# Twelve token-tile pairs by 7 products instead of nine, ScalarE copies for the turns, and row loads behind a landed turn, in an attention and feed-forward kernel on one core

## The chip, the cores and the metric

The kernel runs on one core of a Trainium2 chip. The metric is device time in microseconds (us) of one execution. A core has TensorE (PE: matmuls, into the 8 banks of PSUM), VectorE (DVE), ScalarE (ACT), GpSimd (POOL), SyncE (SP), each with its own in-order queue, and 16 DMA engines that all of them share. SP's queue issues the stores of results and the transposing DMAs, POOL's queue issues the loads.

## The reference

```python
def _attn_ref(q, k, v):            # 8 batches, 12 heads, 448 rows, 64 columns
    scale = 1.0 / np.sqrt(q.shape[-1])
    scores = scale * np.matmul(q, k.transpose(0, 1, 3, 2))
    attn = np.maximum(scores, 0.0) ** 2 / q.shape[2]
    return np.matmul(attn, v)

def _moe_ref(x, w_in, w_out, alpha):   # x: 3584 tokens x 768; w_in 768 x 2048; w_out 2048 x 768
    h = x @ w_in
    g = np.maximum(h, 0.0) + alpha * np.minimum(h, 0.0)
    return g @ w_out
```

The heads' outputs, side by side, are x. All inputs and the result are float32 in memory; the kernel computes in bf16 and sums in float32.

## The kernel before

A **group** n is four heads of one batch (three groups a batch, 24 in all). Its q and k rows are loaded (`load_qk`, L112), its v rows by `load_v` (L121). q and k must be turned, so that the head's 64 columns lie on partitions: groups 0 to 4 by matmuls with the identity (`turn_pe`), groups 5 to 23 by `turn_dma` (L185): two copies put the rows in order into `perm` (one buffer for all; groups 5, 7 and 8 borrow memory of `w_mix`), and one transposing DMA from SP writes T. The copies are made by DVE up to n = 11 and by POOL from n = 12 on (L192, `GP`).

**Scores** of a group come in 7 chunks of two banks each. `sc` (L253) multiplies a chunk (`score_mm`, L206), has its relu taken out of PSUM by ACT ("A", L215) or DVE ("D", L217), and puts the chunk on a list, `late`. `sq(k)` squares the first k of that list on DVE (L228). `attnv(n)` (L231) multiplies all 7 squared chunks with v into two banks; ACT and DVE each take one into xT (L248, L249). `burst(n)` is some chunks of a later group, attnv(n), and some more chunks; PA, PB and PC (L559 to L561) are its patterns of engines, FB is three chunks at ff = 9.

**f1** of a batch b has 16 steps ff: six matmuls of 448 columns (L272), `neg` by ACT (L280, two buffers), gT = neg x beta + h by DVE (L281), and one square from `late`. gT holds the activations of two batches (896 tokens, 7 tiles of 128), `sb` = b // 2 being the number of these two.

**The output** gT @ w_out is made in one of two ways. A *direct* tile, `f2(sb, c, h)` (L298): 16 matmuls of 256 columns for h = 0, 16 of 512 for h = 1, copied out by ACT (L307), stored by SP. A *pair* of tiles, class `Pair` (L320): the 256 tokens x 2048 times 2048 x 768 as a 2 x 2 block product in 7 products (p1 to p7) of 8 matmuls with 384 columns (L340). It needs four mixes S of gT for each pair (`mix`, L336, DVE), four mixes of w_out made once (`weight_mix`, L318, DVE, in halves) and seven drains, five of them sums on DVE (L345), two copies on ACT (p1, p2).

The order is written out by hand. After b = 1 (L608 to L635) come the 7 direct tiles of batches 0 and 1, with score chunks, weight mixes, and bursts 6 to 8 between them. Then the loop over b from 2 to 7 (L638): f1 with the turns of two groups at ff = 1 and 9, then the output stage. For even b that is the pair (0, 1) and the direct tile 2 of its two batches, for odd b the pairs (3, 4) and (5, 6). Between the products stand the three bursts of the batch, and `prepare(n0 + 4)` behind the first of them. `prepare(n)` turns group n and loads all rows of group n + 2.

PSUM banks are given by a counter in program order (`take_bank`, `take_pair`: the least recently taken, from b = 2 on filled pair by pair; `hold` keeps a bank back). A matmul into a bank waits until the bank's last reader is done, so a late DVE or ACT instruction comes back to PE as a wait some banks later.

Of the kernel before, what the change touches and what calls it, by code (L numbers as in the profile page):

```python
# [11 lines left out]
BF16 = mybir.dt.bfloat16  # L12
# [1 line left out]
ALU = mybir.AluOpType  # L14

PP = 64
GP = 12
NJ = 7


# [1 line left out]
def kernel(  # L22
# [28 lines left out]
    rl_pool = ctx.enter_context(tc.tile_pool(name="rl", bufs=6))  # L51
    at_pool = ctx.enter_context(tc.tile_pool(name="at", bufs=10))
    xT_pool = ctx.enter_context(tc.tile_pool(name="xT", bufs=2))
    g_pool = ctx.enter_context(tc.tile_pool(name="g", bufs=1))
    neg_pool = ctx.enter_context(tc.tile_pool(name="neg", bufs=2))
    o_pool = ctx.enter_context(tc.tile_pool(name="o", bufs=6))
    u_pool = ctx.enter_context(tc.tile_pool(name="u", bufs=2))
# [124 lines left out]
            copy = nc.vector.tensor_copy if eng == "D" else nc.scalar.copy  # L182
            copy(dst, ps[:, 128 * lo:128 * hi])  # L183

    def turn_dma(n):  # L185
        if n in (5, 7, 8):
            w = w_mix[2 + n % 2].rearrange("p k c -> p (k c)")[:, :4 * NJ * D]
            p = w.rearrange("p (a j s d) -> p a j s d", a=2, j=NJ, s=2)
        else:
            p = perm_pool.tile([128, 2, NJ, 2, D], BF16, tag="perm", name="perm")  # L190
        for i, name in enumerate("qk"):
            (nc.gpsimd if n >= GP else nc.vector).tensor_copy(p[:, i], raw.pop((n, name)).rearrange("p s j d -> p j s d"))  # L192
        t = T_pool.tile([128, 2, NJ, 128], BF16, tag="T", name="T")
        nc.sync.dma_start_transpose(out=t.rearrange("p a j c -> p (a j) c"),
                                    in_=p.rearrange("p a j s d -> p (a j s d)"))
        T[n] = t
# [68 lines left out]
        sq()  # L265


    gT = {}

    def f1_mm(ps, b, ff, ks):  # L270
        for km in ks:
# [2 lines left out]
                             start=(km == 0), stop=(km == KM - 1))  # L274

    def f1_out(ps, b, ff):
        if b // 2 not in gT:
            gT[b // 2] = g_pool.tile([128, KF, 2 * S], BF16, tag="g", name="gT")
        neg = neg_pool.tile([128, S], F32, tag="neg", name="neg")
        nc.scalar.activation(neg, ps, ACTF.Relu, scale=-1.0)  # L280
        nc.vector.scalar_tensor_tensor(gT[b // 2][:, ff, (b % 2) * S:(b % 2) * S + S],  # L281
                                       neg, beta_sb[:, ff:ff + 1], ps, ALU.mult, ALU.add)
        sq(1)

# [13 lines left out]
    def f2(sb, c, h, parts=None):  # L298

        first_col, width = COLS[h][0], COLS[h][1] - COLS[h][0]  # L300
        o = o_pool.tile([128, d_model - CUT], F32, tag="o", name="osb")
        for lo, hi in parts or ((0, width),):
            ps = take_bank()[:, :hi - lo]
            for ff in range(KF):
                nc.tensor.matmul(ps, gT[sb][:, ff, bass.ts(c, 128)], w_out_sb[:, ff, first_col + lo:first_col + hi],  # L305
                                 start=(ff == 0), stop=(ff == KF - 1))
            nc.scalar.copy(o[:, lo:hi], ps)  # L307
            store(sb, c, first_col + lo, first_col + hi, o[:, lo:hi], nc.scalar if parts else nc.sync)
# [10 lines left out]

    class Pair:  # L320

        def __init__(self, sb, ta, tb):
            self.sb, self.ta, self.tb = sb, ta, tb
            ga, gb = gT[sb][:, :, bass.ts(ta, 128)], gT[sb][:, :, bass.ts(tb, 128)]
            self.a11, self.a12, self.a21, self.a22 = ga[:, :KH], ga[:, KH:], gb[:, :KH], gb[:, KH:]
            self.s = {}

# [30 lines left out]
        def p2(self):  # L358
            self.mm(self.x, self.a12, w_out_sb[:, KH:, :NH], False)
            t = o_pool.tile([128, d_model - CUT], F32, tag="o", name="osb")[:, :NH]  # L360
            nc.scalar.copy(t, self.x)
            take(self.xb, 1)
            store(self.sb, self.ta, 0, NH, t)

        def p6(self):
            y = take_bank()[:, :NH]
# [8 lines left out]
        def p5(self):  # L375
            self.zb = hold()
            self.z = psum[:, self.zb, :NH]
            self.mm(self.z, self.s[1], w_mix[0], True)
            store(self.sb, self.tb, NH, d_model, self.plus(self.z, self.u3))

        def p4(self, parts=((0, NH),)):
            for lo, hi in parts:
                y = take_bank()[:, :hi - lo]
                self.mm(y, self.a22, w_mix[3][:, :, lo:hi], True)
                t = self.plus(y, self.u3[:, lo:hi])
                store(self.sb, self.tb, lo, hi, t, nc.scalar if len(parts) > 1 else nc.sync)

        def p3(self):
            self.mm(self.z, self.s[4], w_out_sb[:, KH:, NH:], False)
            store(self.sb, self.ta, NH, d_model, self.plus(self.z, self.u2))  # L390
            take(self.zb, 1)


# [112 lines left out]
        for ff in range(lo, hi):  # L506
            f1(b, ff)

    def load(n):
        if n < NQ:  # L510
            load_qk(n)
            load_v(n)

    def prepare(n):
        if n < NQ:
            turn_dma(n)
        load(n + 2)

    f1s(0, 4, 6)
    sc(ch(3, 0, 3))  # L520
# [6 lines left out]
    f1_out(ps, 0, 9)  # L527
    f1s(0, 10, 12)
    sc(ch(3, 6, 7) + ch(4, 0, 2, "AA"))
    turn_dma(5)  # L530
    f1s(0, 12, 13)
    kept = late[:]
    del late[:]
# [33 lines left out]
        at_c[0] = min(lo + k, len(chunks))  # L567
        return [(n, j, e) for (n, j), e in zip(chunks[lo:at_c[0]], p)]

    def burst(n, before="ADA", after="AD", squares=True):  # L570

        sc(some(len(before), before))
        attnv(n)
        sc(some(len(after), after))
        if squares:
            sq()

    early = []
    for ff in range(5):
        early.append(hold())  # L580
        f1_mm(psum[:, early[ff], :S], 1, ff, range(4))
        if ff == 1:
            sc(ch(5, 5, 7))
            sq(1)
            sq(1, "A")
        if ff == 3:
            attnv(5)
            turn_dma(6)
            nc.gpsimd.tensor_copy(landed, T[6][:1, 0, 0, :1])
            load_w_out(1, 4)  # L590
            load_qk(9)
            load_v(6)
            load_v(7)
    for ff in range(KF):
        if ff < 5:
            f1_mm(psum[:, early[ff], :S], 1, ff, range(4, KM))
            f1_out(psum[:, early[ff], :S], 1, ff)
            take(early[ff], 1)
        else:
            f1(1, ff)  # L600
        if ff in (1, 10):
            turn_dma(7 + ff // 9)
        if ff == 10:
            nc.gpsimd.tensor_copy(landed, T[8][:1, 0, 0, :1])
            load_v(8)
            load_v(9)
            load(10)
    f2(0, 3, 0)  # L608
    run(some(3))
    f2(0, 4, 0)  # L610
    run(some(3))
    f2(0, 0, 1)
    prepare(9)
    f2(0, 1, 1)
    run(some(3))
    weight_mix(0, 0, 4)
    f2(0, 5, 0)
    burst(6)
    f2(0, 2, 1)
    weight_mix(0, 4, 8)  # L620
    weight_mix(1, 0, 4)
    run(some(3))
    f2(0, 3, 1)
    weight_mix(1, 4, 8)
    f2(0, 6, 0)
    prepare(10)
    burst(7)
    weight_mix(2, 0, 4)
    f2(0, 4, 1)
    weight_mix(2, 4, 8)  # L630
    f2(0, 5, 1)
    weight_mix(3, 0, 4)
    burst(8)
    f2(0, 6, 1)
    weight_mix(3, 4, 8)  # L635

    paired.append(1)
    for b in range(2, B):  # L638
        n0 = NG * (b + 1)
        last = b == B - 1  # L640
        sb = b // 2
        for ff in range(KF):
            if not last:
                if ff in FB:
                    sc(some(*FB[ff]))
                if ff in (1, 9):
                    prepare(n0 + 2 + ff // 8)
            f1(b, ff)
        if b % 2 == 0:
            p = Pair(sb, 0, 1)  # L650
            f2(sb, 2, 0)
            p.mix(1, 2)
            burst(n0, *PA, False)
            p.mix(3)
            p.p1()
            sq(4)
            prepare(n0 + 4)
            p.p6()
            sq(1)
            p.p7()  # L660
            p.mix(4)
            p.p2()
            sq(1)
            p.p5()
            sq(1)
            p.p4()
            p.p3()
            burst(n0 + 1, *PB)
            f2(sb, 2, 1)
            burst(n0 + 2, *PC, False)  # L670
        else:
            p, r = Pair(sb, 3, 4), Pair(sb, 5, 6)
            p.p1()
            p.mix(1, 2)
            r.p1()
            p.mix(3)
            r.mix(1)
            p.p2()
            sq()
            if not last:  # L680
                r.p2()
                burst(n0, *PA, False)
                prepare(n0 + 4)
                sq(3)
            p.p6()
            sq(1)
            p.p7()
            p.mix(4)
            p.p5()
            r.mix(2)  # L690
            p.p4()
            sq(1)
            p.p3()
            if not last:
                burst(n0 + 1, *PB, False)
            r.mix(3)
            sq(2)
            r.p6()
            sq(2)
            r.p7()  # L700
            r.mix(4)
            r.p5()
            if last:
                r.p2()
                r.p3()
                r.p4(((0, 256), (256, 384)))
            else:
                sq(1)
                r.p4()
                sq()  # L710
                r.p3()
                burst(n0 + 2, *PC, False)

# [29 lines left out]
```

## Time and profile before

| | |
|---|---|
| median of 3 runs | 380.89 us (380.72 to 382.02) |
| the profiled execution | 382.1 us, of which 380.1 us from the first to the last instruction (the span) |
| DVE squares L228 | 162, 98.3 us, mean 645 ns |
| DVE gT L281 | 128, 85.3 us, mean 677 ns |
| ACT relu of scores L215 | 135, 115.9 us, mean 929 ns |
| DVE relu of scores L217 | 33, 35.9 us, mean 1088 ns |
| turn copies L192 on DVE | 14, some 613 ns each |
| turn copies L192 on POOL | 24, mean 1011 ns (q) and 1193 ns (k) |
| transposing DMAs, issue to landing | 4.0 / 5.5 / 13.4 us (min, median, max of 19) |
| POOL's waits for T<-perm at L192 | 106.3 us in 12 waits |

The profile page gives for each engine the time that it was busy and its share of the span. A row of a group of instructions is: line, engine, operation, output and inputs, how many, busy time, mean ns of one. The chain of waits follows the work that ended last back from the end: each piece has its start, its length and what it was. A row of the timeline has the start, the length, engine, line and what it wrote and read, and in brackets how long the engine idled before it and for whom. In a table by stage each row has the stretch, its length, and the busy time of PE, PE's weight loads (PEld), DVE, ACT and POOL with the count of instructions, then the granted clock, the DMA share and GB/s. Stretches used below start and end where PE turns from one stage to the next.

### The profile page before, as it was taken

The numbers are of one execution on the slowest core, as the hardware profiler recorded it, in microseconds if no ns is written. First come the engines' busy times: TensorE is split into PE (matmuls) and PEld (weight loads), VectorE is DVE, ScalarE is ACT, GpSimd is POOL, SyncE is SP. The second block draws the span as 40 slices with busy tenths as digits, with TensorE's granted clock in tenths as the row PEclk, the third lists the DMA queues.
The fourth block names the chain that finished last, engine by engine and source line by source line (L and its number), as shares of the span: only waits on it lengthen the run. The fifth ranks groups of instructions, "written<-read, shape, count | busy, mean of one in ns | idle before, by whom it ended". The sixth has DMA issues, their size and how long they took to land.

```text
span 380.1 us, 7810 instructions
## 1 busy us (share of the span) xinstructions
PE 367.7 (97%) x3112; PEld 204.3 (54%) x3112; DVE 288.4 (76%) x466; ACT 217.2 (57%) x339; POOL 94.1 (25%) x129
## 2 busy tenths in 40 slices
PE   7799999999999999999999999999999999999995
PEld 5454564555545455554655546554565546655553
DVE  2997988886988498777688779657879678756752
ACT  4988786556345653856644666576454766364400
POOL 8566050506210434043040430424011000000000
PEclk9999999999999999999999999999999999999999
DMA  9999989999996587859277686747062500220033
GB/s 142 199 203 202 178 132 192 165 195 176 225 178 116 96 135 109 154 92 111 56 130 144 81 117 108 140 93 122 1 96 62 108 2 14 60 53 0 1 85 84
DMA packets 73556, 43.28 MB, mean 114 GB/s; under 512 B 40368, under 2 KB 72240, under 8 KB 73520
## 3 DMA queue, kind: packets, MB, share of 16 engines
q0 software_dynamic: 27136, 22.58, 41.4%
q1 hardware_dynamic: 45952, 19.91, 26.9%
q8 instruction: 24, 0.39, 0.4%
q10 hardware_dynamic: 432, 0.30, 0.3%
q14 instruction: 12, 0.10, 0.1%
HBM read 45.62 MB, written 11.01 MB: 149 GB/s over the span
## 4 chain that ended last, share of the span: by engine, by line
PE 83%; DVE 11%; ACT 3%; issue 2%; POOL 0%; ACTq 0%; POOLq 0%
PE psum L272 31%; PE psum L340 21%; PE psum L305 14%; PE psum L238 9%; PE psum L206 8%; DVE at L228 5%; DVE gT L281 4%; ACT rl L215 2%; PE psum L180 1%; PE psum L164 1%; DVE rl L217 1%; DVE osb L345 1%; ACT xT L248 0%; ACT neg L280 0%; DVE T L183 0%
## 5 line engine op out<-in xcount | busy, mean ns | idle before, releaser
L272 PE MATMUL psum<-xT,w_in_sb 128*128 128x448 bf16 x768 | 148.9, 353 | 0.2
L215 ACT ACTIVATE rl<-psum 128x896 bf16<-128x896 f32 x135 | 115.9, 929 | 31.7 <-PE psum L206 22.4
L281 DVE SCALAR_TENSOR_TENSOR gT<-neg,beta_sb,psum 128x448 bf16<-128x448 f32 x128 | 85.3, 677 | 41.3 <-ACT neg L280 40.2
L272 PEld LDWEIGHTS <-w_in_sb 128*128 128x128 bf16 x768 | 73.9, 98 | 72.2 <-issue 4.8
L280 ACT ACTIVATE neg<-psum 128x448 f32<-128x448 f32 x128 | 68.9, 549 | 57.3 <-PE psum L272 39.8
L228 DVE TENSOR_TENSOR at<-rl 128x896 bf16<-128x896 bf16 x162 | 98.3, 645 | 0.2
L305 PE MATMUL psum<-w_out_sb,gT 128*128 128x256 bf16 (+1 forms) x320 | 54.7, 326 | 0.0
L206 PE MATMUL psum<-T 64*64 64x448 bf16 x672 | 47.6, 359 | 3.5 <-DVE gT L281 1.1
L217 DVE TENSOR_SCALAR rl<-psum 128x896 bf16<-128x896 f32 x33 | 35.9, 1088 | 13.3 <-PE psum L206 11.8
L305 PEld LDWEIGHTS <-gT 128*128 128x128 bf16 x320 | 30.4, 98 | 23.6 <-issue 3.8
L340 PEld LDWEIGHTS <-S 128*128 128x128 bf16 x288 | 28.0, 98 | 19.6 <-issue 1.2
L192 POOL COPY perm<-qraw 128x896 bf16<-128x896 bf16 x12 | 12.1, 1011 | 106.3 <-DMA T<-perm 106.3
L238 PE MATMUL psum<-at,vraw 64*64 64x448 bf16 x672 | 36.9, 350 | 0.8 <-DVE osb L345 0.8
L340 PE MATMUL psum<-w_mix,S 128*128 128x384 bf16 x216 | 37.2, 326 | 0.1
L206 PEld LDWEIGHTS <-T 64*64 64x64 bf16 x672 | 20.0, 106 | 23.5 <-issue 16.7
L238 PEld LDWEIGHTS <-vraw 64*64 64x64 bf16 x672 | 22.9, 106 | 12.4 <-issue 4.6
L340 PEld LDWEIGHTS <-gT 128*128 128x128 bf16 x224 | 21.6, 98 | 14.4 <-issue 0.9
L307 ACT COPY osb<-psum 128x256 f32<-128x256 f32 (+1 forms) x20 | 9.6, 479 | 30.9 <-PE psum L305 30.9
L340 PE MATMUL psum<-w_out_sb,gT 128*128 128x384 bf16 x144 | 25.0, 326 | 0.1
L125 POOL DMA_DIRECT2D vraw<-in_v_dram x24 | 17.4, 727 | 30.4 <-PE psum L206 28.1
L249 DVE TENSOR_SCALAR xT<-psum 128x448 bf16<-128x448 f32 x24 | 15.0, 624 | 11.9 <-PE psum L238 9.1
L345 DVE TENSOR_TENSOR osb<-psum,u 128x384 f32<-128x384 f32 (+2 forms) x28 | 15.2, 543 | 10.9 <-DMA out_dram<-osb 5.1
(44 smaller groups left out, 199.9 us busy)
## 6 DMA issues: line engine op xcount, KB each, us to landing
out_dram<-osb SPq DMA_DIRECT2D x70, 96.0 KB, 2.2
vraw<-in_v_dram POOLq DMA_DIRECT2D x24, 224.0 KB, 8.1
qraw<-in_q_dram POOLq DMA_DIRECT2D x23, 224.0 KB, 5.6
kraw<-in_k_dram POOLq DMA_DIRECT2D x23, 224.0 KB, 7.2
w_in_sb<-in_moe_w_in_dram POOLq DMA_DIRECT2D x16, 192.0 KB, 8.2
out_dram<-osb SPq DMA_DIRECT2D x20, 128.0 KB, 4.1
w_out_sb<-in_moe_w_out_dram POOLq DMA_DIRECT2D x4, 512.0 KB, 9.5
out_dram<-osb SPq DMA_DIRECT2D x21, 64.0 KB, 5.7
```

Of the source, the lines that this page charges most:

```text
L125: nc.gpsimd.dma_start(out=t.rearrange("p m j d -> p m (j d)"), in_=flat[:, 2 * g:2 * g + 2])
L206: nc.tensor.matmul(ps[64 * c:64 * c + 64, r, :S], t[64 * r:64 * r + 64, 1, j, 64 * c:64 * c + 64], t[64 * r:64 * r + 64, 0, :, 64 * c:64 * ...
L215: nc.scalar.activation(rl, ps[:, :, :S], ACTF.Relu)
L217: nc.vector.tensor_scalar(rl, ps[:, :, :S], 0.0, None, ALU.max)
L228: nc.vector.tensor_tensor(a, rl, rl, ALU.mult)
L238: nc.tensor.matmul(ps[64 * s:64 * s + 64, r, :S], vv[64 * r:64 * r + 64, s, j, :], a[64 * r:64 * r + 64, s], start=(j == 0), stop=(j == NJ ...
L272: nc.tensor.matmul(ps, w_in_sb[:, km // 2, km % 2, bass.ts(ff, 128)], xT[b][:, km // 2, km % 2, :], start=(km == 0), stop=(km == KM - 1))
L280: nc.scalar.activation(neg, ps, ACTF.Relu, scale=-1.0)
L281: nc.vector.scalar_tensor_tensor(gT[b // 2][:, ff, (b % 2) * S:(b % 2) * S + S], neg, beta_sb[:, ff:ff + 1], ps, ALU.mult, ALU.add)
L305: nc.tensor.matmul(ps, gT[sb][:, ff, bass.ts(c, 128)], w_out_sb[:, ff, first_col + lo:first_col + hi], start=(ff == 0), stop=(ff == KF - 1))
L340: nc.tensor.matmul(ps, left[:, i], right[:, i], start=(start and i == 0), stop=(i == KH - 1), skip_group_check=not start)
L345: nc.vector.tensor_tensor(t, ps, u, ALU.add)
```

## The change

- gT becomes one tile for the whole kernel, written in place, so that tiles of batch b can still be read while the next batch writes the other half. A `Pair` is now given as two (sb, tile) positions, which may lie in different pairs of batches.
- Twelve pairs instead of nine. Tiles 0, 1, 2 of the first two batches stay direct; (3, 4) and (5, 6) become pairs. The second of these is finished only in the output stage of b = 2: its S mixes are made at ff = 11 to 13, its products p6, p7, p5, p4, p3 come after f1. Every later batch but b = 5 has two pairs, among them one of tile 6 of batches 2 and 3 with tile 0 of batches 4 and 5, and so on; b = 5 has one pair and one direct tile.
- The copies of turns from n = 9 on are made by ACT; those of 5 to 8 stay on DVE. The turns inside f1 move from ff = 1 and 9 to ff = 4 and 12 (turn 8, in b = 1, from ff = 10 to 8).
- `prepare(n)` lets POOL read one element of T(n), so that its queue waits for the turn's landing, and then loads q and k of n + 2 and v of n + 1 (before: q, k and v of n + 2 at once). Around b = 1 loads are put behind turns by hand in the same way.
- Score chunks in the stage after b = 1 change their engines and places (three are moved into f1 of b = 1); squares are moved, among them one between the first chunks and attnv of burst PB (`mid`).

```diff
-GP = 12
...
-    g_pool = ctx.enter_context(tc.tile_pool(name="g", bufs=1))
...
 
-    def turn_dma(n):
+    def turn_dma(n, eng="A"):
         if n in (5, 7, 8):
             w = w_mix[2 + n % 2].rearrange("p k c -> p (k c)")[:, :4 * NJ * D]
             p = w.rearrange("p (a j s d) -> p a j s d", a=2, j=NJ, s=2)
         else:
             p = perm_pool.tile([128, 2, NJ, 2, D], BF16, tag="perm", name="perm")
         for i, name in enumerate("qk"):
-            (nc.gpsimd if n >= GP else nc.vector).tensor_copy(p[:, i], raw.pop((n, name)).rearrange("p s j d -> p j s d"))
+            (nc.vector.tensor_copy if eng == "D" else nc.scalar.copy)(p[:, i], raw.pop((n, name)).rearrange("p s j d -> p j s d"))
         t = T_pool.tile([128, 2, NJ, 128], BF16, tag="T", name="T")
...
-    gT = {}
+    gT = singles.tile([128, KF, 2 * S], BF16, name="gT")
...
     def f1_out(ps, b, ff):
-        if b // 2 not in gT:
-            gT[b // 2] = g_pool.tile([128, KF, 2 * S], BF16, tag="g", name="gT")
         neg = neg_pool.tile([128, S], F32, tag="neg", name="neg")
         nc.scalar.activation(neg, ps, ACTF.Relu, scale=-1.0)
-        nc.vector.scalar_tensor_tensor(gT[b // 2][:, ff, (b % 2) * S:(b % 2) * S + S],
+        nc.vector.scalar_tensor_tensor(gT[:, ff, (b % 2) * S:(b % 2) * S + S],
                                        neg, beta_sb[:, ff:ff + 1], ps, ALU.mult, ALU.add)
...
 
-        def __init__(self, sb, ta, tb):
-            self.sb, self.ta, self.tb = sb, ta, tb
-            ga, gb = gT[sb][:, :, bass.ts(ta, 128)], gT[sb][:, :, bass.ts(tb, 128)]
+        def __init__(self, a, b):
+            self.a, self.b = a, b
+            ga, gb = gT[:, :, bass.ts(a[1], 128)], gT[:, :, bass.ts(b[1], 128)]
             self.a11, self.a12, self.a21, self.a22 = ga[:, :KH], ga[:, KH:], gb[:, :KH], gb[:, KH:]
...
 
-    def load(n):
-        if n < NQ:
-            load_qk(n)
-            load_v(n)
-
     def prepare(n):
         if n < NQ:
             turn_dma(n)
-        load(n + 2)
+            nc.gpsimd.tensor_copy(landed, T[n][:1, 0, 0, :1])
+        if n + 2 < NQ:
+            load_qk(n + 2)
+        if n + 1 < NQ:
+            load_v(n + 1)
 
...
-    turn_dma(5)
+    turn_dma(5, "D")
...
 
-    def burst(n, before="ADA", after="AD", squares=True):
+    def burst(n, before="ADA", after="AD", squares=True, mid=0):
 
         sc(some(len(before), before))
+        sq(mid)
         attnv(n)
...
             attnv(5)
-            turn_dma(6)
+            turn_dma(6, "D")
             nc.gpsimd.tensor_copy(landed, T[6][:1, 0, 0, :1])
             load_w_out(1, 4)
-            load_qk(9)
             load_v(6)
-            load_v(7)
     for ff in range(KF):
...
             f1(1, ff)
-        if ff in (1, 10):
-            turn_dma(7 + ff // 9)
+        if ff == 9:
+            sc(some(3, "AAA"))
+        if ff in (1, 8):
+            turn_dma(7 + ff // 8, "D")
         if ff == 10:
             nc.gpsimd.tensor_copy(landed, T[8][:1, 0, 0, :1])
+            load_qk(9)
+            load_v(7)
+            load_qk(10)
             load_v(8)
-            load_v(9)
-            load(10)
-    f2(0, 3, 0)
-    run(some(3))
-    f2(0, 4, 0)
-    run(some(3))
+    p, r = Pair((0, 3), (0, 4)), Pair((0, 5), (0, 6))
+    p.p1()
+    run(some(3, "AAA"))
+    r.p1()
+    run(some(2, "AD"))
+    p.p2()
+    weight_mix(0, 0, 4)
+    r.p2()
+    weight_mix(0, 4, 8)
     f2(0, 0, 1)
-    prepare(9)
+    weight_mix(1, 0, 4)
+    burst(6, "ADA", "AA", False)
+    turn_dma(9)
+    nc.gpsimd.tensor_copy(landed, T[9][:1, 0, 0, :1])
+    load_qk(11)
+    load_v(9)
+    sq(3)
+    weight_mix(1, 4, 8)
     f2(0, 1, 1)
-    run(some(3))
-    weight_mix(0, 0, 4)
-    f2(0, 5, 0)
-    burst(6)
+    sq()
+    p.mix(1, 2)
+    weight_mix(2, 0, 4)
+    sc(some(3, "AAA"))
+    p.mix(3)
+    weight_mix(2, 4, 8)
     f2(0, 2, 1)
-    weight_mix(0, 4, 8)
-    weight_mix(1, 0, 4)
-    run(some(3))
-    f2(0, 3, 1)
-    weight_mix(1, 4, 8)
-    f2(0, 6, 0)
-    prepare(10)
-    burst(7)
-    weight_mix(2, 0, 4)
-    f2(0, 4, 1)
-    weight_mix(2, 4, 8)
-    f2(0, 5, 1)
+    sq()
+    burst(7, "ADA", "AA", False)
+    turn_dma(10)
+    nc.gpsimd.tensor_copy(landed, T[10][:1, 0, 0, :1])
+    load_qk(12)
+    load_v(10)
+    load_v(11)
     weight_mix(3, 0, 4)
-    burst(8)
-    f2(0, 6, 1)
+    sq(1)
+    p.p6()
     weight_mix(3, 4, 8)
+    sq(1)
+    p.p7()
+    p.mix(4)
+    p.p5()
+    sq(2)
+    p.p4()
+    sq(1)
+    p.p3()
+    burst(8, "ADA", "AAA", False)
 
     paired.append(1)
+    pairs = {3: (((1, 2), (1, 3)), ((1, 4), (1, 5))),
+             4: (((1, 6), (2, 0)), ((2, 1), (2, 2))), 6: (((2, 6), (3, 0)), ((3, 1), (3, 2))),
+             7: (((3, 3), (3, 4)), ((3, 5), (3, 6)))}
     for b in range(2, B):
...
                     sc(some(*FB[ff]))
-                if ff in (1, 9):
+                if ff in (4, 12):
                     prepare(n0 + 2 + ff // 8)
+            if b == 2 and ff == 8:
+                p, r = r, Pair((1, 0), (1, 1))
+            if b == 2 and 11 <= ff <= 13:
+                p.mix(ff - 10)
+            if b == 2 and ff == 14:
+                r.p1()
             f1(b, ff)
-        if b % 2 == 0:
-            p = Pair(sb, 0, 1)
-            f2(sb, 2, 0)
+        if b == 5:
+            p = Pair((sb, 3), (sb, 4))
+            f2(sb, 5, 0)
             p.mix(1, 2)
...
             burst(n0 + 1, *PB)
-            f2(sb, 2, 1)
+            f2(sb, 5, 1)
             burst(n0 + 2, *PC, False)
         else:
-            p, r = Pair(sb, 3, 4), Pair(sb, 5, 6)
-            p.p1()
-            p.mix(1, 2)
-            r.p1()
-            p.mix(3)
-            r.mix(1)
-            p.p2()
-            sq()
+            if b > 2:
+                p, r = [Pair(*t) for t in pairs[b]]
+                p.p1()
+                p.mix(1, 2)
+                r.p1()
+                p.mix(3)
+                r.mix(1)
+                p.p2()
+                sq()
+            else:
+                p.p6()
+                r.mix(1)
             if not last:
                 r.p2()
                 burst(n0, *PA, False)
                 prepare(n0 + 4)
                 sq(3)
-            p.p6()
+            if b > 2:
+                p.p6()
             sq(1)
...
             if not last:
-                burst(n0 + 1, *PB, False)
+                burst(n0 + 1, *PB, False, 1)
             r.mix(3)
...
             else:
-                sq(1)
+                sq(2)
                 r.p4()
-                sq()
                 r.p3()
```

(`store` and `f2` take the one gT and the pair's positions accordingly.)

More of the change, by code (lines that the diff above doesn't have):

```diff
@@ L304, in f2 @@
             for ff in range(KF):
-                nc.tensor.matmul(ps, gT[sb][:, ff, bass.ts(c, 128)], w_out_sb[:, ff, first_col + lo:first_col + hi],
+                nc.tensor.matmul(ps, gT[:, ff, bass.ts(c, 128)], w_out_sb[:, ff, first_col + lo:first_col + hi],
                                  start=(ff == 0), stop=(ff == KF - 1))
@@ L362, in p2 @@
             take(self.xb, 1)
-            store(self.sb, self.ta, 0, NH, t)
+            store(*self.a, 0, NH, t)
         def p6(self):
@@ L378, in p5 @@
             self.mm(self.z, self.s[1], w_mix[0], True)
-            store(self.sb, self.tb, NH, d_model, self.plus(self.z, self.u3))
+            store(*self.b, NH, d_model, self.plus(self.z, self.u3))
         def p4(self, parts=((0, NH),)):
@@ L385, in p4 @@
                 t = self.plus(y, self.u3[:, lo:hi])
-                store(self.sb, self.tb, lo, hi, t, nc.scalar if len(parts) > 1 else nc.sync)
+                store(*self.b, lo, hi, t, nc.scalar if len(parts) > 1 else nc.sync)
         def p3(self):
             self.mm(self.z, self.s[4], w_out_sb[:, KH:, NH:], False)
-            store(self.sb, self.ta, NH, d_model, self.plus(self.z, self.u2))
+            store(*self.a, NH, d_model, self.plus(self.z, self.u2))
             take(self.zb, 1)
```

## The prediction

> **What bounds the kernel now.** I read the busy times first, then the chain of waits from b=2 on, then busy time by stage, then single squares on VectorE.
>
> ```profile
> PE 367.7 (97%) x3112; PEld 204.3 (54%) x3112; DVE 288.4 (76%) x466; ACT 217.2 (57%) x339; POOL 94.1 (25%) x129
> PEclk9999999999999999999999999999999999999999
> ```
>
> TensorE (PE) works 367.7 of 380.1 us at the full granted clock. A busy PE need not be a useful PE, so I look at what it issues, in the chain of waits (start, length, what):
>
> ```profile
> 138.29 1.75 PE psum L305 x16
> ...
> 142.68 9.26 PE psum L340 x56
> ...
> 154.67 3.56 PE psum L305 x16
> ...
> 165.77 0.59 DVE gT L281
> 166.36 0.68 DVE at L228
> 167.04 0.59 DVE gT L281
> 167.63 0.54 DVE at L228
> ```
>
> Columns run at a fixed rate: 16 matmuls of 256 columns take 1.75 us, 16 of 512 take 3.56, 56 of 384 take 9.26 (0.165 each). A **direct** token tile costs 1.75 + 3.56 = 5.31, two cost 10.62, a **pair by 7 products** 9.26. The chain passes through VectorE (DVE) only in places: from 163.9 to about 172 it alternates gT and squares at 1.13 us per ff, beside six matmuls of 1.147 us. So PE sets the time, and DVE runs so close that each delay of it can show. The stages show where it does (length; busy PE, PEld, DVE, ACT, POOL):
>
> ```profile
> 76.53:119.17 42.64, 42.22 (x370) 22.06 (x368) 35.19 (x52) 21.03 (x31) 10.22 (x15) 1.00 1.20 189
> 119.17:138.13 18.96, 18.96 (x110) 9.57 (x109) 13.56 (x23) 10.96 (x19) 6.66 (x8) 1.00 0.55 99
> 138.13:161.05 22.92, 22.84 (x246) 13.74 (x245) 18.75 (x29) 13.82 (x21) 6.30 (x8) 1.00 0.77 132
> 161.05:181.05 20.00, 19.52 (x109) 9.77 (x108) 14.88 (x25) 12.57 (x21) 7.48 (x9) 1.00 0.77 105
> 181.05:208.63 27.58, 26.88 (x270) 16.21 (x268) 23.12 (x38) 13.99 (x21) 5.00 (x6) 1.00 0.58 109
> ...
> 271.16:298.15 26.99, 26.68 (x269) 16.14 (x267) 22.38 (x38) 13.99 (x21) 2.60 (x2) 1.00 0.39 70
> 298.15:317.51 19.36, 19.36 (x110) 9.81 (x110) 13.96 (x25) 12.55 (x21) 0.00 (x0) 1.00 0.17 35
> 317.51:338.90 21.39, 21.37 (x222) 12.56 (x220) 15.96 (x27) 11.62 (x17) 0.00 (x0) 1.00 0.19 44
> ```
>
> They are: the direct tiles after b=1; f1 and output of b=2; f1 and output of b=3; output of b=5; f1 and output of b=6. The same f1 with squares takes 20.0 in b=3 and 19.36 in b=6, the one in which POOL copies nothing.
>
> **Parts 1 and 2: the pairs.** Three direct pairs of tiles become 7-product pairs: 3 x (10.62 - 9.26) = **4.1 us of PE** less. It is moved work too. After b=1 go 4 x 1.75 + 7 x 3.56 = 31.9 and come 3 x 3.56 + 72 products x 0.165 = 22.6, so -9.3. b=2 has 96 products (40 left from the carried pair, 56 of its own) for 56 and a direct tile: 15.9 - 14.6 = +1.3. b=4 and b=6 trade a direct tile for a pair, +3.95 each; b=5 does the opposite, -3.95. Sum -4.1 again.
>
> DVE gains 12 S mixes x 0.687 and 15 sums x 0.557 = 16.6 us; six drains of scores (relu) that turn from D to A in the stage after b=1 take 6 x 1.088 = 6.5 off, three turns that leave it 6 x 0.613 = 3.7. Net +6.4 before part 3.
>
> Stage by stage, taking each new stage from one of its kind in this trace:
> - After b=1: 42.64 - 9.3 = 33.3. DVE: four weight_mix pairs 7.6, 27 squares less 3 and 6 that move into f1 = 18 x 0.62 = 11.2, four drains 4.4, xT 1.9, four mixes 2.7, five sums 2.8: 30.6, beside 33.3. It fits on the whole, but the last third doesn't: from burst(7) the sums, the last two mixes of weights and squares come one after another, while the products are 1.3 us each; burst(8)'s attnv waits for a square and a bank. Laid out in order I get about 1 us of waiting: **34.3**.
> - b=2: f1 18.96 plus r.p1 (1.3) plus 0.3 for squares that it lacked: 20.6. Output: the b=5 one less the three products not there, 26.99 - 3.9 = 23.1, plus 0.5 because gT of ff 15 comes later (three mixes at ff 11 to 13, turn copies at ff 12) and r.p2 waits for it: **44.2**.
> - b=3, b=4: f1 19.4, output 27.0 each: **92.8**.
> - b=5: 19.4 + 22.9 = **42.3**.
> - b=6: 19.4 + 27.0 less 1.5 for the scores that have run out (22.92 - 21.39): **44.9**.
>
> Together 258.5 against 338.90 - 76.53 = 262.4 before: **-3.9 us**. b=7 and all before b=1 is as it was.
>
> **Part 3: turn copies, from POOL (n >= 12) and DVE (n = 9 to 11) to ACT.** Thirty copies. ACT shows no SBUF copy of this size; the nearest row is its square of 128x896 bf16, 1009 ns; I take 1.0, so 2.0 a turn, at most 30 us on 217 (with six drains and the pairs about 250 of 376, 66%). Does ACT's queue delay anything? At ff=4 the neg of ff=4 waits behind them, then gT, then PE's bank. But neg already waits for gT two back, which runs at 1.13 us per ff: about 2.8 us between the end of one gT and the start of the third after it, against 0.55 + 2.0 + 0.55 = 3.1. It costs DVE 0.3, in the time before ff 6 to 8 where DVE has no squares. At ff=12 the copies come on top of three drains (ff 9, 2.5 us); nothing but neg is behind, and gT of ff 15 is due 3.7 us later (p1, r.p1, half of p2): nothing, except in b=2 (above). After PA, ACT is idle 4.65 us before PB: nothing. Without that cover the price is 2 us x 15 turns.
>
> What leaves is POOL's hold on DVE:
>
> ```profile
> 164.37 0.93 POOL L192 COPY perm<-qraw 128x896 bf16<-128x896 bf16 x1 [9.25 <-DMA T<-perm]
> ```
> ```profile
> 164.49 1.28 DVE L228 TENSOR_TENSOR at<-rl 128x896 bf16<-128x896 bf16 x1
> ...
> 167.56 0.61 DVE L228 TENSOR_TENSOR at<-rl 128x896 bf16<-128x896 bf16 x1
> ```
>
> A square beside the copy takes 1.28, the next without one 0.61. The Trainium skill, SBUF — State Buffer, section "SBUF: two separate sides", says that the pair of ports shared by DVE and GpSimd is locked for a whole instruction and the loser stops. By that rule 24 copies of some 1.1 us take up to 26 us from DVE. The rows give less: squares in b=2 to b=5, each stage against the same one of b=6 (0.62 and 0.56 each), lose 4.3 us in all, as DVE is waiting or reading PSUM for much of the time. On the end it is less still: PE's score group at ff=9 of b=3 lasts 1.74 us instead of 0.69, of b=6 0.94; that, and a square of 1.35 us ahead of PB, is what "19.4" above gives back. By the rule another 10 us could be hoped for; I go by the rows.
>
> **Part 4: rows fetched once a turn has landed.** `landed` on POOL waits for T, and load_qk(n+2), load_v(n+1) are behind it on POOL, which has nothing else left. SP's transpose now waits for ACT's copies instead of POOL's; stores behind it are freed sooner after PA (up to 5.4 us of POOL's wait for the buffer stood there). Landing of a transpose: median 5.5 us; 8.7 to 13.4 between 68 and 120 us with loads ahead of it, 4.0 to 8.2 afterwards. The Trainium skill, DMA: Bandwidth & Descriptors, section "Rules for kernel authors", speaks against the wait: issue DMAs early, and a transpose beside ordinary transfers needs nothing. By it the wait only makes rows later, by 4 to 6 us; by the rows it makes T earlier by up to 8. Either is hidden if rows land in time: from ff=4, 2.0 + 5 + 1.5 + 6 = 14.5 us, needed at the turn after PA, some 22 us later. After b=1 it is tight: T(8) lands near 82, rows 9 near 89, their turn near 90. Both 0 for the sum; the bounds go into the range (-0.5 to +2).
>
> **Sum.** The profiled execution took 382.1: span 380.1 and 2.0 around it. Span 376.2, that execution 378.2. It was 1.2 above the median of 380.89 (runs 380.72 to 382.02), so the forecast is 380.9 - 3.9 = **377.0**.
>
> **Rivals.**
> - *All of the waits go too.* PE's minimum says more than 4.1: score groups at ff=9 lose 1.05, 0.5, 1.0, 0.25 us over 0.69; outputs of odd batches lose 1 to 1.5. With POOL quiet some 2 to 3 us of these go beside the 4.1: **374.5**. For it: b=6's f1. Against: DVE's +6.4, and four stages with two pairs in place of two.
> - *DVE becomes the bound.* In the outputs with two pairs DVE is busy 22.4 to 23.1 us of 27, and the order of its queue, not its sum, sets PE's waits. If each of the new ones (b=2, 4, 6) and the stage after b=1 lose 0.8 more: +3.2, **380.2**, no difference.
> - *ACT waits for the transpose.* One perm buffer: a turn's copies wait until the last transpose has read it. On POOL that wait (106 us in all) stood beside nothing; on ACT, neg and drains are behind it. It decides once a transpose lands more than 7.8 us after issue: ff 4 to ff 12 is 9.9 us, less 2.0 for copies and 0.1. At 13.4, ACT stands 5.6 us, PE's banks cover some 3.4, 2.2 are lost in each of b=2 to b=6: +11, **388**. At 10 to 11, still 2 to 4 above the forecast. Against it: landings after 120 us are 4.0 to 8.2, and with the load behind it the 4.0 end is likelier.
> - *gT as one tile orders what it needn't*, if a write waits for readers of other columns. psum is also one tile and its banks run independently; counted within the second.
>
> **Chances.** Forecast 0.60, all waits 0.14, DVE 0.16, ACT 0.10. 0.5% (1.9 us) is about what a measurement of this kernel can tell from no change. Faster: the first two and a small part of the third, 0.77; same 0.13; slower 0.10. Low end: below 374.5 PE would need to lose nearly every wait; high end: the DVE case.
>
> **What would show it.** PE's busy sum falls by 4 to 5 us; L305 has 128 matmuls, L340 680 (8 more, as the last p4 goes in two parts). Squares have no 1.3 us outliers. Stage after b=1 near 34, b=2 near 44. Score groups at ff=9 near 0.95. ACT's wait for "DMA T<-perm" is near zero; if it isn't, or outputs of b=2, 4, 6 are over 28 us, the forecast is wrong.

## The result and the profile after

The changed kernel takes **375.62 us** (median of 4 runs, 375.11 to 376.17), the kernel before 381.45 (4 runs): ratio 0.9845, 95% interval 0.9812 to 0.9878. It is 5.8 us faster; the forecast was 3.9. A second comparison on another occasion gave 375.96 against 381.83, ratio 0.9842 (0.9821 to 0.9863). One execution each of e1 and e5 below took over 950 us (in e1's a matmul of f1 took 758 ns at the median instead of 352) and is left out.

The profiled execution has a span of 374.4 us, 5.7 less. Busy times of the changed kernel, to be read against the row of before:

```profile
PE 364.6 (97%) x3085; PEld 203.2 (54%) x3088; DVE 289.0 (77%) x481; ACT 242.1 (65%) x369; POOL 72.4 (19%) x120
```

PE still works at 97%. Of PEld, whose records are complete, there are 24 fewer, eight for each of three pairs. ACT has 25 us more, POOL 22 less, and DVE is where it was: what the three pairs gave it, the drains, the turns and POOL's silence took.

Busy time by stage, columns as before. The rows are the stage after b=1; f1 and output of b=2; f1 and output of b=3; f1 and output of b=5; f1 and output of b=6:

```profile
77.77:110.88 33.11, 32.65 (x300) 16.80 (x301) 28.63 (x44) 22.80 (x33) 8.57 (x14) 1.00 0.99 167
110.88:131.45 20.57, 20.57 (x116) 10.44 (x116) 15.53 (x28) 16.02 (x26) 4.03 (x7) 1.00 0.85 133
131.45:154.35 22.90, 22.84 (x246) 14.06 (x244) 20.36 (x35) 14.17 (x20) 5.04 (x8) 1.00 0.74 134
154.35:173.63 19.28, 19.28 (x108) 9.67 (x108) 13.91 (x25) 15.49 (x25) 2.33 (x4) 1.00 0.48 80
173.63:200.55 26.92, 26.80 (x270) 16.23 (x269) 22.61 (x38) 15.65 (x23) 4.66 (x8) 1.00 0.72 133
246.75:266.03 19.28, 19.28 (x108) 9.66 (x108) 13.91 (x25) 15.48 (x25) 2.33 (x4) 1.00 0.45 75
266.03:288.95 22.92, 22.80 (x244) 13.73 (x244) 17.82 (x29) 15.49 (x23) 3.22 (x6) 1.00 0.70 124
288.95:308.24 19.29, 19.29 (x109) 9.67 (x109) 13.89 (x25) 14.04 (x23) 0.18 (x1) 1.00 0.14 27
308.24:333.74 25.50, 25.44 (x245) 15.20 (x244) 20.95 (x36) 11.67 (x17) 0.00 (x0) 1.00 0.22 52
```

Each f1 of b=3 to b=6 is now 19.28 or 19.29; before, from PE's first matmul of f1 to its first of the output, they were 20.0, 19.5, 20.0 and 19.2. Set against the lengths of before:

| stage | before | after | difference | forecast |
|---|---|---|---|---|
| all before b=2 | 119.17 | 110.88 | -8.3 | -8.3 |
| b=2 | 41.9 | 43.5 | +1.6 | +2.3 |
| b=3 | 47.6 | 46.2 | -1.4 | -1.2 |
| b=4 | 42.4 | 46.2 | +3.8 | +4.0 |
| b=5 | 47.1 | 42.2 | -4.9 | -4.8 |
| b=6 | 40.7 | 44.8 | +4.1 | +4.2 |
| b=7 and the end | 41.2 | 40.7 | -0.6 | 0 |
| sum | | | -5.7 | -3.9 |

Work has moved as laid out: 8.3 us leave the front, 8 come back in b=4 and b=6. The sum is 1.8 us better than forecast, 0.7 of it in b=2 and 0.6 in b=7, whose instructions the change leaves in their order. This table adds up but doesn't say which edit did what, as every stage has several of them. That is what the runs are for.

### The profile page after: what moved, and what is told of

It reads as the page before. It is cut to its first block, busy times and chain, and to the rows that moved or that the text cites. A ratio compares the mean times of both kernels' runs of the same rounds, so it can differ in the third digit from the quotient of the medians.

```text
span 374.4 us, 7851 instructions
## 1 busy us (share of the span) xinstructions
PE 364.6 (97%) x3085; PEld 203.2 (54%) x3088; DVE 289.0 (77%) x481; ACT 242.1 (65%) x369; POOL 72.4 (19%) x120
## 4 chain that ended last, share of the span: by engine, by line
PE 68%; ACT 2%; DVE 1%; issue 0%; DVEq 0%
PE psum L270 29%; PE psum L336 26%; PE psum L236 6%; PE psum L204 5%; PE psum L301 1%; ACT xT L246 1%; DVE osb L341 0%; ACT rl L213 0%; DVE at L226 0%; DVE u L341 0%; DVE S L332 0%; DVEq L341 0%
## 5 line engine op out<-in xcount | busy, mean ns | idle before, releaser
L213 ACT ACTIVATE rl<-psum 128x896 bf16<-128x896 f32 x141 | 120.4, 925 | 35.6 <-PE psum L204 35.6
L277 DVE SCALAR_TENSOR_TENSOR gT<-neg,beta_sb,psum 128x448 bf16<-128x448 f32 x128 | 85.3, 678 | 41.2 <-ACT neg L276 40.0
L276 ACT ACTIVATE neg<-psum 128x448 f32<-128x448 f32 x128 | 68.0, 550 | 40.7 <-PE psum L270 33.1
L336 PEld LDWEIGHTS <-S 128*128 128x128 bf16 x384 | 37.2, 98 | 26.7 <-issue 2.7
L336 PE MATMUL psum<-w_mix,S 128*128 128x384 bf16 x288 | 49.2, 326 | 0.2
L336 PEld LDWEIGHTS <-gT 128*128 128x128 bf16 x296 | 28.5, 98 | 19.1 <-issue 0.9
L215 DVE TENSOR_SCALAR rl<-psum 128x896 bf16<-128x896 f32 x27 | 29.4, 1090 | 10.1 <-PE psum L204 8.6
L336 PE MATMUL psum<-w_out_sb,gT 128*128 128x384 bf16 x192 | 33.2, 326 | 0.0
L341 DVE TENSOR_TENSOR osb<-psum,u 128x384 f32<-128x384 f32 (+2 forms) x37 | 20.2, 546 | 8.7 <-PE psum L336 3.9
L301 PE MATMUL psum<-w_out_sb,gT 128*128 128x256 bf16 (+1 forms) x125 | 21.7, 325 | 0.2
L357 ACT COPY osb<-psum 128x384 f32<-128x384 f32 x12 | 5.7, 479 | 20.9 <-PE psum L336 20.9
L246 ACT ACTIVATE xT<-psum 128x448 bf16<-128x448 f32 x24 | 13.2, 549 | 8.0 <-PE psum L236 7.3
```

The source lines that it names most:

```text
L213: nc.scalar.activation(rl, ps[:, :, :S], ACTF.Relu)
L215: nc.vector.tensor_scalar(rl, ps[:, :, :S], 0.0, None, ALU.max)
L277: nc.vector.scalar_tensor_tensor(gT[:, ff, (b % 2) * S:(b % 2) * S + S], neg, beta_sb[:, ff:ff + 1], ps, ALU.mult, ALU.add)
L301: nc.tensor.matmul(ps, gT[:, ff, bass.ts(c, 128)], w_out_sb[:, ff, first_col + lo:first_col + hi], start=(ff == 0), stop=(ff == KF - 1))
L336: nc.tensor.matmul(ps, left[:, i], right[:, i], start=(start and i == 0), stop=(i == KH - 1), skip_group_check=not start)
L341: nc.vector.tensor_tensor(t, ps, u, ALU.add)
```

## The experiments

Differences are against the kernel before, in us: of the medians, on the same chip, and of the profiled executions from PE's first matmul of f1 of b=1 to the end (323.87 us before). The second leaves out a start that is the same in all of these kernels and yet took from 55.2 to 56.3 us; behind it two executions of the changed kernel took 318.07 and 318.08 us. "FB" is the time from the start of PE's score group at ff 9 of b=3 to the next matmul of f1; the least for its 12 matmuls is 0.69 us.

| run | pairs | turn copies | turns at ff | wait for landing | medians | profile from b=1 on | FB |
|---|---|---|---|---|---|---|---|
| before | 9 | POOL | 1, 9 | no | 0 | 0 | 1.74 |
| e1, e1b | 9 | ACT | 1, 9 | no | +3.4 | +3.3 (e1b) | 1.92 (e1b) |
| e8 | 9 | ACT | 4, 12 | no | -2.8 | -2.1 | 1.02 |
| e2 | 12 | POOL | 1, 9 | no | -2.1 | -2.5 | 1.60 |
| e3 | 12 | ACT | 4, 12 | no | -5.2 | -4.8 | 1.02 |
| changed | 12 | ACT | 4, 12 | yes | -5.8, -5.9 | -5.8, -5.8 | 1.02 |
| e5 | 12 | POOL | 4, 12 | yes | -1.1 | -1.9 | 1.65 |
| e4 | 12 | ACT | 1, 9 | yes | -0.4 | -0.1 | 1.91 |
| e6 | 12 | DVE | 4, 12 | yes | +2.9 | +3.4 | 1.99 |

In the profiles the parts add up: the pairs bring 2.5 us (e2) or 2.7 (e3 against e8), the copies with their place 2.1 (e8) or 2.3 (e3 against e2), and the wait for the landing 1.0 (the changed kernel against e3).

### The pairs alone (e2)

```diff
-            (nc.vector.tensor_copy if eng == "D" else nc.scalar.copy)(p[:, i], ...)
+            (nc.vector.tensor_copy if eng == "D" else nc.gpsimd.tensor_copy if n >= 12 else nc.scalar.copy)(p[:, i], ...)
-            nc.gpsimd.tensor_copy(landed, T[n][:1, 0, 0, :1])        # in prepare
-                if ff in (4, 12):
+                if ff in (1, 9):
```

> The changed kernel's twelve pairs with turn copies of n >= 12 on POOL, prepare without the wait for the landing, and turns at ff 1 and 9. If the pairs bring PE's 4.1 us and nothing else: 3.5 to 4.5 us less than before (ratio 0.988 to 0.991). If DVE, with POOL's copies beside it and four stages of two pairs, eats it up: 1 to 3 us less only. If the pairs make all of the 5.8: 5.5 or more less.

Measured: 2.1 us less (ratio 0.9951, 0.9936 to 0.9965), 2.5 in the profile. This is the second case: some 40 to 50% of PE's 4.1 us is given back. With the pairs come, in e2 too, the other order of the stage after b=1, v rows fetched one turn later and ACT's copies for n = 9 to 11; these weren't parted. The output of b=2 in this kernel shows one place where time is lost:

```profile
132.34:156.17 23.83, 23.00 (x245) 13.98 (x244) 21.75 (x35) 12.50 (x18) 8.66 (x10) 1.00 0.95 148
```

It takes 23.83 us, where the changed kernel takes 22.90 for the same work of PE. DVE is busy 21.75 us against 20.36 with as many instructions (35). Two of them make most of the difference, a mix of 1.15 us in place of 0.68 and a square of 1.35 in place of 0.62 (the first of two in the second row), beside POOL's copies at 145.53 and 146.40:

```profile
145.85 1.15 DVE L332 TENSOR_TENSOR S<-gT 128x1024 bf16<-128x1024 bf16 x1
146.92 1.88 DVE L226 TENSOR_TENSOR at<-rl 128x896 bf16<-128x896 bf16 x2
```

### The copies, their engine and their place (e1, e8, e5, e4, e6)

e1 and e8 put only the copies of n >= 12 on ACT in the kernel before; e8 moves the turns as well:

```diff
-            (nc.gpsimd if n >= GP else nc.vector).tensor_copy(p[:, i], ...)
+            (nc.scalar.copy if n >= GP else nc.vector.tensor_copy)(p[:, i], ...)
-                if ff in (1, 9):                  # e8 alone
+                if ff in (4, 12):
```

> The kernel before with the turn copies of n >= 12 on ACT instead of POOL; nine pairs, turns at ff 1 and 9, loads as before. If POOL's copies held DVE up and that reached PE: 0.7 to 2.2 us less than before (ratio 0.994 to 0.998), squares without the 1.3 us ones, PE's score groups at ff 9 of b=3 and b=5 about 1.0 us instead of 1.7. If the pairs alone make the gain: within 0.3 us of before. If ACT's queue is the dearer place (ff 1 is where ACT still has three drains to catch up): 1 us or more slower.

> The same kernel as e1_copies_alone, for a profile of an undisturbed run (e1 took 385.2, 3.5 us more than before). If the place at ff 1 is the cause (ACT still has three drains of the last burst to do): gT of ff 1 and the following come 1.5 to 2 us later than in the kernel before, and PE waits at ff 9, FB 2.5 us or more. If a late transpose is the cause (rows loaded ahead of it): ACT's copies at ff 9 or after PA wait for T<-perm, over 1 us each.

> The kernel before with turn copies of n >= 12 on ACT, at ff 4 and 12 instead of 1 and 9; loads still at once, nine pairs. If the place at ff 1 cost e1 its 3.5 us: 0.5 to 2 us less than before. If the late transposes did: as e1, 2 to 4 us more than before.

e1 was 3.4 us **slower** (ratio 1.0097, 1.0082 to 1.0111), the third case. e8 was faster, by 2.8 us in the medians; but the interval of its ratio (0.9949, 0.9930 to 0.9968) allows only 1.2 to 2.7, and the profile gives 2.1. From b=2 on e1b takes 264.2 us and e8 258.8: the same copies, on the same engine, are worth 5.4 us more or less by their place. ACT at the start of f1 of b=3 in e1b (start, length):

```profile
163.67 0.94 ACT L215 ACTIVATE rl<-psum 128x896 bf16<-128x896 f32 x1
164.47 0.58 ACT L280 ACTIVATE neg<-psum 128x448 f32<-128x448 f32 x1
164.90 0.97 ACT L192 COPY perm<-qraw 128x896 bf16<-128x896 bf16 x1
165.72 0.98 ACT L192 COPY perm<-kraw 128x896 bf16<-128x896 bf16 x1
166.56 1.02 ACT L280 ACTIVATE neg<-psum 128x448 f32<-128x448 f32 x2
```

PE began this f1 at 162.24. ACT's first neg comes 2.2 us later, as three drains of the last burst lie in front of it, and the two copies keep the second back till 166.56. From there DVE alternates gT and squares at 1.13 us a step against PE's 1.147, so it carries the delay on to ff 9, where PE's scores want the banks. PE in e1b, then in e8:

```profile
172.54 0.57 PE L206 MATMUL psum<-T 64*64 64x448 bf16 x8
173.55 0.38 PE L206 MATMUL psum<-T 64*64 64x448 bf16 x2 [0.44 <-DVE gT L281]
174.15 0.38 PE L206 MATMUL psum<-T 64*64 64x448 bf16 x2 [0.22 <-DVE gT L281]
```
```profile
170.42 1.09 PE L206 MATMUL psum<-T 64*64 64x448 bf16 x12
```

In e1b the group is broken by two waits for gT; in e8 it is one piece. No copy of e1b waited for a transpose, so the second of the two explanations falls. The first holds, but not in its numbers: FB is 1.92, not 2.5 or more. Against the kernel before, whose long square beside POOL's copy does the same harm in b=3 (FB 1.74), e1b loses elsewhere: at ff 9 of b=4 and b=6 (1.91 for 1.22 and 0.94), and in the outputs of b=2 and b=4, which begin with a direct tile that soon reads gT of ff 15 (23.97 and 23.70 us for 22.92).

The same two edits in the changed kernel, one at a time, and all copies on DVE:

```diff
                if ff in (4, 12):          # e4: (1, 9)
        ... nc.gpsimd.tensor_copy if n >= 12 ...     # e5: the copies as in e2
        ... nc.vector.tensor_copy(p[:, i], ...)      # e6
```

> The changed kernel with its turns inside f1 at ff 1 and 9 again; copies on ACT, wait for the landing kept. If the place is what counts: 2 to 4 us slower than the changed kernel, FB 1.5 to 2.5 us in b=2 to b=6. If it is the landing: within 0.5 us of the changed kernel.

> The changed kernel with the turn copies of n >= 12 on POOL again; wait for the landing and turns at ff 4 and 12 kept. POOL's lock on DVE as cause of what exceeds 4.1: 1 to 2 us slower than the changed kernel (3.8 to 4.8 less than before), squares of 1.3 us back, groups at ff 9 above 1.02. If the copies' engine doesn't matter: within 0.4 us of the changed kernel (5.4 to 6.2 less than before).

> The changed kernel with all turn copies on DVE (0.61 us each, 1.2 a turn, 18 us on DVE in all), ACT free of them. If DVE's queue is what stands behind PE: 2 to 5 us slower than the changed kernel, FB 1.3 us or more, outputs of two pairs over 27.2. If ACT's copies cost as much as they save: within 0.5 us or faster.

e4 ends level with the kernel before (0.4 us under it, ratio 0.9993, 0.9982 to 1.0004): the place alone costs 5.4 us (5.7 in the profile, where 2 to 4 were expected), nearly all of the gain. e5 keeps 1.1 (0.9967, 0.9952 to 0.9981), 4.7 us worse than the changed kernel (3.9 in the profile), more than I had expected even of the theory that I held. It isn't the mirror of e8: with the wait kept, POOL's next copies stand in its queue behind a landing and the loads after it, as below, and e2, with POOL's copies at ff 1 and 9 and no wait, does better. e6 is 2.9 us slower than before (1.0085, 1.0061 to 1.0110), 8.7 us behind the changed kernel and beyond the 2 to 5 expected, although a DVE copy takes 0.61 us and an ACT copy 0.93: the stage after b=1 loses 2.5 us (b=2 starts at 113.4 instead of 110.9), FB is 1.99. Its outputs of two pairs take 27.13 us, not over 27.2.

What POOL's copies do to DVE, in e5 near the end of f1 of b=5 (POOL, then DVE):

```profile
265.10 0.72 POOL L123 DMA_DIRECT2D vraw<-in_v_dram  x1
265.81 0.95 POOL L190 COPY perm<-qraw 128x896 bf16<-128x896 bf16 x1
266.69 0.94 POOL L190 COPY perm<-kraw 128x896 bf16<-128x896 bf16 x1
```
```profile
266.01 2.11 DVE L226 TENSOR_TENSOR at<-rl 128x896 bf16<-128x896 bf16 x1
268.04 0.67 DVE L277 SCALAR_TENSOR_TENSOR gT<-neg,beta_sb,psum 128x448 bf16<-128x448 f32 x1
```

The square starts 0.2 us after the first copy and ends 0.5 us after the second: 2.11 us in place of 0.62. It stood still for nearly all of both. Of the 1.5 us that DVE lost, PE then waits 0.59 us for gT in the output behind it.

### The wait for the landing (e3)

```diff
         if n < NQ:
             turn_dma(n)
-            nc.gpsimd.tensor_copy(landed, T[n][:1, 0, 0, :1])
```

> The changed kernel with prepare's wait for the landing of T taken out, so that rows are loaded as soon as POOL gets there. By my sum 0 (5.4 to 6.2 less than before), with transposes landing after 5 to 8 us in place of 4. If ACT's copies are caught by a late transpose (over 7.8 us): 1 to 5 us slower than the changed kernel, and ACT shows waits for the transpose. If early loads are worth something: faster than the changed kernel.

Measured 5.2 us less than before (ratio 0.9869, 0.9854 to 0.9884), some 0.7 us behind the changed kernel. The intervals overlap, so the medians don't settle it; in the profile it is 1.0 us, 0.6 of it in the output of b=2 and 0.4 behind PE's last product. Transposes after 112 us land in 4.0 / 7.3 / 11.0 us (min, median, max), with the wait in 4.0 / 4.0 / 4.8. The 11.0 is caught by ACT in b=2. ACT of e3 at ff 12, then PE at r.p2 of the same batch:

```profile
128.66 0.94 ACT L190 COPY perm<-qraw 128x896 bf16<-128x896 bf16 x1 [2.62 <-DMA T<-perm]
129.50 0.93 ACT L190 COPY perm<-kraw 128x896 bf16<-128x896 bf16 x1
```
```profile
134.19 0.34 PE L336 MATMUL psum<-w_out_sb,gT 128*128 128x384 bf16 x1 [0.42 <-DVE gT L277]
```

The one perm buffer makes ACT stand 2.62 us for the transpose before it; gT of ff 15 is late, and p2's last product, which reads it, waits 0.42. The output of b=2 takes 23.52 instead of 22.90. This is the third rival's mechanism and the second case, once, and small.

### What was left: two runs on ACT's start, one on a square (e9, e11, e7)

FB of 1.02 in the changed kernel is still 0.33 over its least, in five batches, and no idle time stands before it: the wait is inside "busy". In f1 DVE's first gT shows this in the changed kernel:

```profile
157.19 0.68 DVE L277 SCALAR_TENSOR_TENSOR gT<-neg,beta_sb,psum 128x448 bf16<-128x448 f32 x1 [2.77 <-ACT neg L276]
```

Beside the next two runs stands the changed kernel again, on the same chip:

> The changed kernel itself, as the measure for the next two on the same chip: 5.3 to 6.3 us less than before.

```diff
-    PC = ("ADA", "AAA")            # e9; burst(8) likewise
+    PC = ("ADA", "ADA")
-            burst(n0 + 1, *PB, False, 1)      # e7; the last sq(2) becomes sq(3)
+            burst(n0 + 1, *PB, False)
```

> The changed kernel with the middle one of the three drains behind attnv in the last burst of each batch (PC, and burst 8) on DVE instead of ACT. In the changed kernel's f1 DVE stands 2.8 us until ACT has done three drains and the first neg, and PE's score group at ff 9 takes 1.02 us where 0.69 is its least. If ACT's late start is what is left at ff 9: FB 0.7 to 0.8 us in b=2 to b=6, 1.0 to 1.8 us faster than the changed kernel. If DVE can't take the drain (1.09 us): within 0.5 us of it, or slower.

> The changed kernel without the square that was put ahead of attnv in burst PB (mid); it is made behind the next mix instead. If DVE's order there counts: 0.5 to 1.5 us slower than the changed kernel, outputs of two pairs 27.1 us or more in place of 26.9. If it only fills an idle place of DVE: within 0.3 us.

c: 375.96. e9: 375.68 (ratio to before 0.9840, 0.9818 to 0.9861), the same. DVE's first wait fell from 2.77 to 0.97 us, but FB stayed at 1.00 to 1.01. e7: 376.23, the same within its spread (0.3 us more in the profile); outputs of two pairs are 27.00 instead of 26.92: that square does little but fill an idle place of DVE.

So the late start alone wasn't what bound. In e9 DVE waits again, 0.8 us, behind the two copies at ff 4:

```profile
161.74 0.68 DVE L277 SCALAR_TENSOR_TENSOR gT<-neg,beta_sb,psum 128x448 bf16<-128x448 f32 x1 [0.79 <-ACT neg L276]
```

In the changed kernel gT of ff 0 starts 1.55 us behind PE's last matmul for it, and gT of ff 4 1.60; in e9 it is 0.74 and 1.59. Either cause makes DVE equally late at ff 4, so taking one away shows nothing. e11 is e9 with the first turn of each f1 split:

```diff
+                if ff == 3 and n0 + 2 < NQ:
+                    begin_turn(n0 + 2)         # perm, and the copy of q
-                if ff in (4, 12):
+                if ff in (5, 12):              # the copy of k and the transpose
```

> e9_drain_on_dve with the first turn of each f1 split: q's copy at ff 3, k's at ff 5, where one copy of 0.93 us stands against some 0.6 us that ACT idles in each step. e9 started DVE 2 us sooner and FB stayed at 1.0, which I put down to the two copies at ff 4 making DVE late again (0.8 us idle behind neg there). If so: no idle of DVE over 0.5 us behind neg at ff 3 to 6, FB 0.7 to 0.8, 1.0 to 1.7 us faster than the changed kernel (6.8 to 7.5 less than before). If FB's 1.0 is of another cause: within 0.4 us of e9.

**374.3 us** (373.4 to 374.5), ratio 0.9804 (0.9791 to 0.9817), 7.4 us less than before, as the first case had it. Of the changed kernel's two intervals (from 0.9812 and from 0.9821 on) the first overlaps this one, the second doesn't; the profile from b=1 on is 1.6 us shorter, five times the 0.33 that FB has lost. FB of e11 and its f1 of b=3:

```profile
163.45 0.76 PE L212 MATMUL psum<-T 64*64 64x448 bf16 x12
```
```profile
153.14:172.09 18.95, 18.95 (x108) 9.62 (x108) 14.94 (x26) 14.75 (x24) 2.33 (x4) 1.00 0.50 78
```

FB is 0.69, f1 18.95 in place of 19.28. ACT has the same work as in e9. One copy of 0.93 us in a step meets some 0.6 us of idle time and is made good in the next: gT of ff 4 starts 0.75 us behind PE, and DVE doesn't wait for neg at ff 3 to 6. Two in a row reach DVE. Whether the split alone, without the drain on DVE, does as much wasn't tried; the 1.55 us at ff 0 speak against it.

## The prediction, point by point

**The pairs.** The forecast's -3.9 held some 2 us that it got from quieter f1s and outputs (19.4 for 20.00, 19.48, 20.13 and 19.36; 27.0 for 27.58), so by its own terms the pairs were worth some -2. e2 measured -2.1, -2.5 in the profile. The price of a pair from the chain of waits, and the 1 us of waiting after b=1, were right: b=2 starts 8.3 us sooner, as laid out. That the sums meet is in part luck: in e2 b=2 takes 45.3 us, 1.1 over its forecast, and b=3 and b=5 make up for it. The 0.5 us that r.p2 was to wait in b=2 came only in e3, where the transposes were late.

**The copies.** "By the rule another 10 us could be hoped for; I go by the rows": the rows gave some 2 us, and moved alone (e8) the copies brought 2.1 in the profile. So this term was right. DVE's busy time fell from 288.4 to 284.9 us in e8, with the same 466 instructions: of the rule's 26 us of stopped DVE, 3.5 show as longer instructions, near the 4.3 that the prediction read from the squares. e5's 4.7 don't measure this term, as they hold the wait in POOL's queue too.

**ACT as the new place.** An ACT copy takes 0.93 us (I took 1.0). "It costs DVE 0.3, in the time before ff 6 to 8 where DVE has no squares" was wrong. In the changed kernel the copies at ff 4 push gT from 1.53 to 1.60 us behind PE, as the late start has made it late already; in e9, where it is punctual, they make DVE wait 0.8. And the delay does reach PE, as FB's 1.02, until the drain is moved and the copies are split: in b=2 and b=6 FB rose from 0.69 and 0.94. I weighed ff 4 and never asked what ff 1 would have cost; e4 says 5.4 us. The change of place, in the diff two digits, is worth more than the pairs.

**The wait for the landing.** This is the term that was mis-sized most. It was put at 0 with -0.5 to +2; measured about -0.7 in the medians, -1.0 in the profile. The mechanism by which it helps was written down as the third rival, but its size there (2.2 us in each of five batches) didn't come: one wait of 2.62 us of ACT in e3, 0.4 of PE, 0.6 in the length of b=2. The other 0.4, at the end, is open. By the rule that a transpose beside ordinary transfers needs nothing the wait could only cost; here it paid. What else exceeds the forecast, 0.9 us (e3's -4.8 for -3.9), is spread over the stages; f1 of 19.28 in place of 19.4 in four batches is half of it.

**The rivals.** "All of the waits go too" was nearest with -6.4 and its reason is the right one in part: POOL's quiet, with the turns at ff 4, took FB down in b=3 to b=5, to 1.02 from 1.74, 1.22 and 1.71. It didn't go all the way; e11 shows the 0.33 us in each of five batches that stayed. DVE as the bound came only with the copies on DVE (e6).

**The signs named.** No square over 0.9 us: so (before it was five of 162). Stage after b=1 near 34 (33.1, and 1.2 more in f1 of b=1), b=2 near 44 (43.5): so. Score groups at ff 9 near 0.95: 1.02. No wait of ACT for the transpose, no output over 28 us: so. 680 matmuls of the pairs: so; of the direct tiles 125 are on record and three missing. PE's sum was to fall by 4 to 5 us and fell by 3.1: its busy time holds waits, so this was a poor sign.

b=7's 0.6 us are open: 22.5 us from the last f1 to the end in all seven kernels with the wait for the landing and copies off POOL, 22.9 to 23.1 in the other six. PE's work is the same; the last store is issued 1.2 us behind PE's end in the changed kernel and 1.5 to 1.6 in before, e3 and e5. No run took this apart.

## What to carry to other kernels

Before moving work from a stalling engine to an idle one, look at what is *behind* the moved instruction at each place it could stand: by their place alone the same copies, 2 us a turn, made this kernel 3.3 us slower or 2.1 faster. Cut such work to pieces that the idle time of a step or two makes good: in e11, two pieces apart cost PE nothing that shows, together they had cost it 0.33 us in each of five batches. When taking one cause of lateness away changes nothing, a second one as large may stand behind it (e9). And an engine at 97% busy can hide waits inside "busy": compare the length of the same group in a stage where nothing disturbs it.

## What the runs showed that I had not expected

A DVE square beside two POOL copies that follow each other waited for both, once, in e5 (2.11 us for 0.62). In the prediction's lines it waits for the first alone (1.28), and in the kernel before POOL's second copy is the longer one there (1.33 us for 0.93). And transposing DMAs with ordinary loads on their way land in 4.0 to 11.0 us, with the loads held back in 4.0 to 4.8.
